# Attention in four query groups of 144 on eight array tiles, with PSUM divided by hand into one region for each stage

## The chip, the cores and the metric

The kernel runs on one core of a Trainium2 chip. The metric is the device time of one execution in microseconds (us). TensorE (PE) multiplies matrices and writes PSUM; VectorE (DVE) and ScalarE (ACT) read PSUM and compute elementwise; GpSimd (POOL) works on SBUF alone; SyncE's queue (SP) starts the DMAs. Each engine works through its own instructions in order and waits at semaphores for the others.

## The reference

Eight batches of eight heads, 576 positions, 64 values a head. Heads 0 to 3 see the 32 positions up to their own, heads 4 to 7 every fourth of the last 128. The attention's output, 4608 rows of 512, goes through a block of two matrix products:

```python
scores = scale * np.matmul(q, k.transpose(0, 1, 3, 2))
scores = np.where(masks[None, :, :, :], scores, -1000000000.0)
attn = softmax(scores)                      # exp, sum, divide
x = (attn @ v).transpose(0, 2, 1, 3).reshape(B * S, H * D)
h = x @ w_in                                # 4608 x 1024
solu = h * softmax(h)
ln = (solu - mean) / sqrt(var + 1e-06) * g_ln
out = ln @ w_out                            # 4608 x 512
```

## The kernel before, in words

**Units and steps.** Attention is cut into 32 units (`n`), two heads of one batch each; units 0 and 1 of a batch have plain heads, units 2 and 3 dilated ones, whose positions the host has regrouped by their remainder modulo 4, so that both kinds need 32 queries against 64 keys at a time. The second block is cut into 36 tiles (`i`) of 128 rows. Units 0 to 3 and the conversion of the weights (float64 bits to two float32r parts, hi and lo) run in a start-up whose order is written out by hand for all engines (`TICKS`). Then come 36 steps, one for each tile. In a step PE computes for tile i `h` (L277, 24 matmuls of 512 columns), for the unit of the step before the product with the values (`attend`, L235), for a new unit the scores (L163), then for tile i-1 the output product `o` (L351, 24 matmuls), and last the eight transposes of tile i (L336). Only PE's order is written by hand in the steps (`LEADS` for the first five, `STEP` for the others); on DVE, ACT and POOL a scheduler places the instructions. A batch is four and a half tiles, so of every nine steps seven have both an `attend` and new scores, one has an `attend` alone and one has scores alone. In steps 2, 5 to 11, 14 to 20 and 23 to 29, 22 in all, the `attend` stands ahead of the scores; steps 31 to 35 have no attention.

**One tile of the second block.** `nmax` (DVE, L288) is the row maximum of `h`, `e` (ACT, L291) the exponential, `t` and `mu` (DVE, L298) their product with `h` and its sum, `t` less its mean follows (L306, L307), and PE transposes it. `th` (ACT, L338) and `tl` (DVE, L339) are the two float32r parts that `o` multiplies. `ob` (ACT, L360) scales the output by `rstd`, which POOL works out in six small instructions (L314 to L321) from two sums.

**One unit of attention.** Queries are stored block-diagonal by head (64 columns for 32 queries of two heads), so one scores matmul has 128 rows, 64 columns of weights and 64 moving columns; 18 of them fill 576 columns in two PSUM tiles (`ps_s0`, `ps_s1`), and two at a time fall on the two halves of the array's columns. DVE adds the mask and takes the maximum (L171, L187), POOL subtracts it (L188), ACT exponentiates (L202), DVE sums, inverts, multiplies (L204 to L214) and transposes blocks of 32 (`pt`, L221). Units 2, 3 and 4 add the mask on PE (L156) and exponentiate straight from PSUM (L197). `attend` has 40 matmuls of 32 rows, 64 columns of weights and up to 64 moving columns, on four tiles of the array, into two PSUM tiles, `ps_x` and `ps_t1`; `ps_t1` is also the tile of the second half of the transposes. `spread` splits each of the two into `x_hi` (ACT, L257) and `x_lo` (DVE, L258), the rows of `h`'s operand.

**PSUM.** Its eight banks hold eight tiles: two for `ps_h`, one each for `ps_o`, `ps_t0`, `ps_t1`, `ps_x`, `ps_s0`, `ps_s1`. A step's waits follow from which instruction reads or writes which of them.

Of the kernel before, what the change touches and what calls it, by code (L numbers as in the profile page):

```python
# [19 lines left out]
NPAIR = H // 2  # L20
# [7 lines left out]
NU = S // WIN // 2  # L28
WQ = 2 * WIN
NV = NU + 1  # L30
KPAD = WIN
RING = 2 * S
HALF = S // 2
# [35 lines left out]
def windowed_attention_then_solu_kernel(  # L69
# [20 lines left out]
    ps_a = ctx.enter_context(tc.tile_pool(name="ps_a", bufs=1, space=PSUM))  # L90
    ps_m = ctx.enter_context(tc.tile_pool(name="ps_m", bufs=1, space=PSUM))
# [9 lines left out]
    mask_sb = const.tile([P, 2, NU, WQ], BF16, name="mask_sb")  # L101
# [8 lines left out]
    x_lo = const.tile([P, KT, RING], F32R, name="x_lo")  # L110
    nc.vector.memset(mhalf, -0.5)
# [28 lines left out]
    def scores(n, part):  # L140

        qt, kt = loaded[n]["q"], loaded[n]["k"]
        dil = int(n % NPAIR >= NPAIR // 2)
        if part == 0:
            st[n] = {"sm": att.tile([P, NU, WQ], F32, name="sm")}
        sm = st[n]["sm"]
        us = range(0, 5) if part == 0 else range(5, NU)
        nu = len(us)
        on_pe = n in PE_MASK
        ps = ps_a.tile([P, 512], F32, name=f"ps_s{part}")  # L150
        ps = ps[:, 0 : 5 * WQ].rearrange("p (u w) -> p u w", w=WQ)
        st[n]["ps", part] = ps
        mk = mask_sb[:, dil, us[0] : us[0] + nu, :]
        if on_pe:
            for c in range(0, P, 64):
                nc.tensor.matmul(  # L156
                    out=ps[c : c + 64, 0:nu, :], lhsT=id_bf[:, c : c + 64], rhs=mk,
                    start=True, stop=False,
                )
        for i, u in enumerate(us):  # L160
            for par in range(2):
                qb = NU * par + u
                nc.tensor.matmul(  # L163
                    out=ps[64 * par : 64 * par + 64, i, :],
                    lhsT=qt[:, qb, :],
                    rhs=kt[:, WIN * qb : WIN * qb + WQ],
                    start=not on_pe,
                    stop=not on_pe or i == nu - 1,
                )
        if not on_pe:  # L170
            nc.vector.tensor_tensor(  # L171
                out=sm[:, us[0] : us[0] + nu, :], in0=ps[:, 0:nu, :], in1=mk, op=ALU.add
            )

    def soft_max(n):
        sm = st[n]["sm"]
        mx = small.tile([P, NU], F32, name="mx")
        if n in PE_MASK:
            st[n]["mx"] = mx
            for part, (u0, u1) in enumerate(((0, 5), (5, 9))):  # L180
                nc.vector.tensor_reduce(
                    out=mx[:, u0:u1], in_=st[n]["ps", part][:, 0 : u1 - u0, :],
                    axis=AX.X, op=ALU.max, negate=True,
                )
# [26 lines left out]
    def soft_norm(n):  # L211
        sm, rs = st[n]["sm"], st[n]["rs"]
        eng = nc.gpsimd if n < NPAIR + POOL_NORM else nc.vector
        eng.tensor_tensor(  # L214
            out=sm, in0=sm, in1=rs.unsqueeze(2).broadcast_to([P, NU, WQ]), op=ALU.mult
        )

    def probs_t(n):

        pt = st[n]["pt"] = att.tile([P, NU * WQ], F32, name="pt")  # L220
        nc.vector.transpose(out=pt, in_=st[n]["sm"].rearrange("p u w -> p (u w)"))  # L221

    def attend(n):

        vt = loaded[n]["v"]
        pt = st[n]["pt"]
        b, pr = divmod(n, NPAIR)
        out = [ps_a.tile([P, 512], F32, name="ps_x"), ps_m.tile([P, 512], F32, name="ps_t1")]
        for i in range(NV):
            u0, u1 = max(i - 1, 0), min(i + 1, NU)  # L230
            k0, k1 = max(WQ * i - WIN, 0), min(WQ * i + WIN, NU * WQ)
            for par in range(2):
                for h in range(2):
                    r = 64 * par + 32 * h
                    nc.tensor.matmul(  # L235
                        out=out[par][64 * h : 64 * h + 64, WIN * u0 : WIN * u1],
                        lhsT=vt[r : r + WIN, i, :],
                        rhs=pt[r : r + WIN, k0:k1],
                        start=i == 0,
                        stop=i == NV - 1,  # L240
                        skip_group_check=True,
                    )
        for half in range(2):
            spread(n, out[half][:, 0:HALF], half)

    def spread(n, ps, half):
        b, pr = divmod(n, NPAIR)
        base = (b % 2) * S

        def view(x):  # L250
            x = x[:, pr, base : base + S]
            if pr < NPAIR // 2:
                return x[:, half * HALF : half * HALF + HALF]
            return x.rearrange("p (i c) -> p c i", c=DIL)[:, 2 * half : 2 * half + 2, :]

        src = ps if pr < NPAIR // 2 else ps.rearrange("p (c i) -> p c i", c=2)
        nc.scalar.copy(out=view(x_hi), in_=src)  # L257
        nc.vector.tensor_tensor(  # L258
            out=view(x_lo), in0=src, in1=view(x_hi).bitcast(F32), op=ALU.subtract
        )  # L260
        if half == 1:
            del st[n], loaded[n]
# [4 lines left out]
    def moe_h(i, half, kts):  # L267
        if half == 0 and kts[0] == 0:
            ms[i] = {"h": ps_m.tile([P, 2, 512], F32, name="ps_h")}
        h = ms[i]["h"]  # L270
# [14 lines left out]
    def moe_act(i):  # L285
        h = ms[i]["h"].rearrange("p a b -> p (a b)")
# [7 lines left out]
    def moe_gate(i):  # L294
        h = ms[i]["h"].rearrange("p a b -> p (a b)")
# [28 lines left out]
    def moe_t():  # L324
# [144 lines left out]
    def front_ops(n):  # L469
        return {  # L470
            "s0": lambda: scores(n, 0),
            "s1": lambda: scores(n, 1),
# [75 lines left out]
def _mask():  # L548
    m = np.full((P, 2, NU, WQ), NEG, np.float32)
    c = np.arange(WQ)  # L550
    for u in range(NU):
        for p in range(P):
            qb = NU * (p // 64) + u
            q = WIN * qb + p % WIN
            k = WIN * (qb - 1) + c
            ok = (k >= 0) & (q - k >= 0) & (q - k < WIN)
            m[p, 0, u, ok] = 0.0
            m[p, 1, u, ok & (k // CLS == q // CLS)] = 0.0
    return m
# [47 lines left out]
```

## Time and profile before

| | |
|---|---|
| median of three runs (lowest to highest) | 576.47 us (576.36 to 577.3) |
| the profiled execution, its span | 577.16 us, 575.1 us |
| mean granted clock of TensorE | 0.967 |
| step with attend and scores, from one nmax to the next | 14.49 or 14.5 us |
| step with attend alone, with scores alone, without attention | 13.29, 13.57, 11.77 us |
| start of the first nmax (end of the start-up) | 61.58 us |

Of the engines' rows: a start, a duration, the engine, the line, the operation, what is written and from what, the shape, and in brackets the idle time ahead of it with what ended it. A matmul's duration includes its way through the array, so matmuls overlap and the distance of their starts tells the rate. The profile merges neighbours ("x36"). A matmul in float32 stands in the trace as two instructions. A table by windows gives for each stretch its length and then, engine by engine, the busy time and the number of instructions, last the granted clock of TensorE, the share of the DMA engines and GB/s.

### The profile page before, as it was taken

How to read it: one execution, taken by the hardware profiler on the slowest of the kernel's cores; microseconds unless marked ns; L12 is line 12 of the kernel's file. 1: busy time of each engine (PE TensorE's matmuls, PEld its weight loads, DVE VectorE, ACT ScalarE, POOL GpSimd, SP SyncE). 2: the span in 40 equal slices, each digit the busy share in tenths (PEclk: the TensorE clock that was granted, in tenths of full speed). 3: DMA queues.
4: the chain of work that ended last, by engine and by line, in shares of the span. 5: the costliest groups of instructions: out<-in, count | busy, mean ns of one | idle time of the engine just before them, and what ended most of it. 6: DMA issues, size and time to landing. Idle time of an engine off the chain costs nothing.

```text
span 575.1 us, 13371 instructions
## 1 busy us (share of the span) xinstructions
PE 531.8 (92%) x5740; PEld 442.2 (77%) x5740; DVE 356.7 (62%) x617; ACT 225.5 (39%) x451; POOL 153.9 (27%) x280
## 2 busy tenths in 40 slices
PE   3464859999999999999999999999999999999996
PEld 2353648888888888888888888888888888888885
DVE  4988995645666666655666666646666666634342
ACT  3467753343333333333333333333333333333232
POOL 2654771212222222211222222211222222211111
PEclk9966779999999999999999999999999999999999
DMA  8786620312333333323232333222333310001000
GB/s 316 233 305 248 200 73 34 106 61 88 103 106 104 105 104 99 103 58 98 96 110 95 106 105 106 98 83 81 114 105 103 96 49 19 19 19 38 18 19 36
DMA packets 22090, 58.40 MB, mean 102 GB/s; under 512 B 2704, under 2 KB 3088, under 8 KB 22032
## 3 DMA queue, kind: packets, MB, share of 16 engines
q1 hardware_dynamic: 22032, 57.55, 30.1%
q8 instruction: 45, 0.74, 0.5%
q14 instruction: 13, 0.11, 0.0%
HBM read 48.11 MB, written 9.44 MB: 100 GB/s over the span
## 4 chain that ended last, share of the span: by engine, by line
PE 83%; DVE 8%; ACT 3%; issue 2%; DMA 2%; POOL 1%; SPq 0%; ACTq 0%; DVEq 0%
PE ps_h L277 34%; PE ps_o L351 32%; PE ps_x L235 5%; PE ps_s L163 5%; PE ps_t L336 5%; DVE mag L399 1%; PE ps_t L235 1%; DVE nmax L288 1%; DVE mag L414 1%; DMA raw<-w_out 1%; DMA mask_sb<-mask 1%; ACT e L291 1%; POOL sm L188 1%; DVE rs L204 1%; DVE mag L407 1%
## 5 line engine op out<-in xcount | busy, mean ns | idle before, releaser
L277 PE MATMUL ps_h<-wi_hi,x_hi 128*128 128x512 f32 x288 | 117.6, 408 | 7.5 <-ACT x_hi L257 5.3
L351 PE MATMUL ps_o<-wo_hi,th 128*128 128x512 f32 x288 | 116.2, 404 | 0.8 <-ACT th L338 0.8
L277 PE MATMUL ps_h<-wi_hi,x_lo 128*128 128x512 f32 x288 | 114.2, 397 | 0.0
L277 PE MATMUL ps_h<-wi_lo,x_hi 128*128 128x512 f32 x288 | 113.7, 395 | 0.0
L351 PE MATMUL ps_o<-wo_hi,tl 128*128 128x512 f32 x288 | 113.1, 393 | 0.0
L351 PE MATMUL ps_o<-wo_lo,th 128*128 128x512 f32 x288 | 113.1, 393 | 0.0
L291 ACT ACTIVATE e<-ps_h,nmax 128x1024 f32<-128x1024 f32 x36 | 40.2, 1116 | 168.2 <-DVE nmax L288 168.2
L288 DVE TENSOR_REDUCE nmax<-ps_h 128x1 f32<-128x1024 f32 x36 | 44.0, 1223 | 81.2 <-PE ps_h L277 81.1
L298 DVE CUSTOM_DVE_ANT_0 t<-ps_h,e 128x1024 f32<-128x1024 f32 x36 | 44.1, 1224 | 41.9 <-ACT e L291 41.9
L277 PEld LDWEIGHTS ps_h<-wi_hi,x_hi 128*128 128x128 f32 x288 | 55.3, 192 | 18.5 <-ACT x_hi L257 6.0
L235 PEld LDWEIGHTS ps_x<-pt,vt 32*64 32x64 f32 x1280 | 44.1, 145 | 31.6 <-issue 19.8
L235 PE MATMUL ps_x<-pt,vt 32*64 32x64 f32 (+1 forms) x1280 | 47.7, 230 | 20.8 <-DVE pt L221 11.4
L314 POOL TENSOR_SCALAR se<-se 128x1 f32<-128x1 f32 x36 | 8.9, 246 | 214.9 <-ACT e L291 214.8
L202 ACT ACTIVATE sm<-sm 128x576 f32<-128x576 f32 x29 | 19.9, 685 | 117.5 <-POOL sm L188 117.5
L351 PEld LDWEIGHTS ps_o<-wo_hi,th 128*128 128x128 f32 x288 | 54.5, 189 | 13.4 <-ACT th L338 1.1
L277 PEld LDWEIGHTS ps_h<-wi_hi,x_lo 128*128 128x128 f32 x288 | 54.9, 190 | 12.7 <-DVE x_lo L258 1.0
L188 POOL TENSOR_TENSOR sm<-sm,mx 128x576 f32<-128x576 f32 x29 | 43.9, 1515 | 75.8 <-DVE mx L187 75.5
L351 PEld LDWEIGHTS ps_o<-wo_hi,tl 128*128 128x128 f32 x288 | 54.5, 189 | 12.0 <-DVE tl L339 0.4
L277 PEld LDWEIGHTS ps_h<-wi_lo,x_hi 128*128 128x128 f32 x288 | 55.3, 192 | 10.2
L351 PEld LDWEIGHTS ps_o<-wo_lo,th 128*128 128x128 f32 x288 | 54.5, 189 | 10.5
L339 DVE TENSOR_TENSOR tl<-ps_t,th 128x512 fp32r<-128x512 f32 x72 | 45.6, 672 | 25.5 <-ACT th L338 25.5
L163 PE MATMUL ps_s<-kt,qt 128*64 128x64 f32 x1152 | 45.9, 239 | 9.8 <-DMA qt<-qT 9.8
(60 smaller groups left out, 756.1 us busy)
## 6 DMA issues: line engine op xcount, KB each, us to landing
qt<-qT SPq DMA_DIRECT2D x32, 576.0 KB, 5.4
vt<-vw SPq DMA_DIRECT2D x32, 320.0 KB, 3.2
kt<-kT SPq DMA_DIRECT2D x32, 304.0 KB, 3.9
out<-ob SPq DMA_DIRECT2D x36, 256.0 KB, 2.0
raw<-w_in SPq DMA_DIRECT2D x8, 512.0 KB, 5.6
raw<-w_out SPq DMA_DIRECT2D x8, 512.0 KB, 4.3
mask_sb<-mask SPq DMA_DIRECT2D x2, 144.0 KB, 5.6
id_sb<-ident SPq DMA_DIRECT2D x1, 64.0 KB, 6.8
```

The source lines that it names most:

```text
L163: nc.tensor.matmul(out=ps[64 * par : 64 * par + 64, i, :], lhsT=qt[:, qb, :], rhs=kt[:, WIN * qb : WIN * qb + WQ], start=not on_pe, stop=n ...
L188: nc.gpsimd.tensor_tensor(out=sm, in0=sm, in1=mx.unsqueeze(2).broadcast_to([P, NU, WQ]), op=ALU.subtract)
L202: nc.scalar.activation(out=sm, in_=sm, func=AF.Exp, scale=0.125)
L235: nc.tensor.matmul(out=out[par][64 * h : 64 * h + 64, WIN * u0 : WIN * u1], lhsT=vt[r : r + WIN, i, :], rhs=pt[r : r + WIN, k0:k1], start= ...
L277: nc.tensor.matmul(out=h[:, half, :], lhsT=a[:, kt, xs], rhs=w[:, kt, ws], start=(kt == 0 and k == 0), stop=(kt == KT - 1 and k == 2),)
L288: nc.vector.tensor_reduce(out=nmax, in_=h, axis=AX.X, op=ALU.max, negate=True)
L291: nc.scalar.activation(out=e, in_=h, func=AF.Exp, bias=nmax, scale=1.0, accum_out=se)
L298: nc.vector.tensor_tensor_reduce(out=t, in0=h, in1=ms[i]["e"], scale=1.0, scalar=0.0, op0=ALU.mult, op1=ALU.add, accum_out=mu,)
L314: nc.gpsimd.tensor_scalar(out=se, in0=se, scalar1=1e-9, scalar2=None, op0=ALU.add)
L336: nc.tensor.transpose(out=ps[:, f, :], in_=t[:, k * P : k * P + P], identity=id_sb)
L339: nc.vector.tensor_tensor(out=tl[:, fs], in0=ps, in1=th[:, fs].bitcast(F32), op=ALU.subtract)
L351: nc.tensor.matmul(out=o, lhsT=a[:, f, :], rhs=w[:, f, :], start=(f == 0 and k == 0), stop=(f == FT - 1 and k == 2),)
```

## The change

**Attention in four groups.** The 576 queries of a head are cut into four groups of 144 (`GQ`), each in five blocks of 32 (`NS`; the last one is half padding), and group c lies on partitions 32c to 32c+31. Queries are stored dense. A scores matmul now has 64 rows (one head), 32 columns of weights and 64 moving columns; there are 40 in a unit, eight at a time on eight tiles of the array (two heads by four groups). `attend` has 48 matmuls of 32 rows in a plain unit and 40 in a dilated one, on eight tiles (four groups by two heads). Arrays of a unit's probabilities grow from 576 to 640 columns. Mask addition, maximum and `spread` become one instruction each where there were two. The loads of a unit are 296 KB of queries (were 576), 312 KB of keys (were 304) and 384 KB of values (were 320).

**PSUM.** One tile of all eight banks is divided by hand. `ps_h` has banks 0 and 1, `ps_o` bank 2, the first half of the transposes bank 3. The second half has columns 0 to 255 of banks 4 and 5, the scores columns 0 to 319 of banks 6 (first head) and 7 (second head), and `ps_x` columns 320 to 463 of banks 4 to 7, one bank for each group. `attend` no longer writes a tile of the transposes.

```diff
-NU = S // WIN // 2
+NG = P // WIN
+GQ = S // NG
+NS = -(-GQ // WIN)
+NV = NS + 1
+SPAN = GQ * (NG - 1) + WIN * NS
...
+    banks = psum.tile([P, 8, 512], F32, name="banks")
+    ps_h = banks[:, 0:2, :]
+    ps_o = banks[:, 2, :]
+    ps_s = banks[:, 6:8, 0 : NS * WQ]
+    ps_x = banks[:, 4:8, NS * WQ : NS * WQ + GQ]
+    ps_t = (
+        banks[:, 3:4, :].rearrange("p b (f q) -> p b f q", q=P),
+        banks[:, 4:6, 0 : 2 * P].rearrange("p b (f q) -> p b f q", q=P),
+    )
...
-        for i, u in enumerate(us):
-            for par in range(2):
-                qb = NU * par + u
-                nc.tensor.matmul(
-                    out=ps[64 * par : 64 * par + 64, i, :],
-                    lhsT=qt[:, qb, :],
-                    rhs=kt[:, WIN * qb : WIN * qb + WQ],
...
+        for i in range(NS):
+            for h in range(2):
+                for c in range(NG):
+                    q0 = GQ * c + WIN * i
+                    nc.tensor.matmul(
+                        out=ps[WIN * c : WIN * c + WIN, h, WQ * i : WQ * i + WQ],
+                        lhsT=qt[D * h : D * h + D, q0 : q0 + WIN],
+                        rhs=kt[D * h : D * h + D, q0 : q0 + WQ],
...
-        out = [ps_a.tile([P, 512], F32, name="ps_x"), ps_m.tile([P, 512], F32, name="ps_t1")]
...
+            for c in range(NG):
                 for h in range(2):
-                    r = 64 * par + 32 * h
                     nc.tensor.matmul(
-                        out=out[par][64 * h : 64 * h + 64, WIN * u0 : WIN * u1],
-                        lhsT=vt[r : r + WIN, i, :],
-                        rhs=pt[r : r + WIN, k0:k1],
+                        out=ps_x[D * h : D * h + D, c, c0 : c0 + k1 - k0],
+                        lhsT=vt[WIN * c : WIN * c + WIN, i, D * h : D * h + D],
+                        rhs=pt[WIN * c : WIN * c + WIN, h, k0:k1],
...
-        for half in range(2):
-            spread(n, out[half][:, 0:HALF], half)
+        spread(n)
...
-        nc.scalar.copy(out=view(x_hi), in_=src)
+        nc.scalar.copy(out=view(x_hi), in_=ps_x)
         nc.vector.tensor_tensor(
-            out=view(x_lo), in0=src, in1=view(x_hi).bitcast(F32), op=ALU.subtract
+            out=view(x_lo), in0=ps_x, in1=view(x_hi).bitcast(F32), op=ALU.subtract
         )
```

**PE in a step.** The rows are the end of an `attend`, the scores and the start of `o` in a step of the middle of the program; in brackets stand the semaphores that an instruction waits for (DMAHW are those of loads). Before:

```order
L235 MATMUL ps_x<-pt,vt 64x32 x2
L235 MATMUL ps_t_3153<-pt,vt 64x32 x2
L163 MATMUL ps_s_3199<-kt,qt 64x64 [waits DMAHW1_49,DMAHW0_49]
L163 MATMUL ps_s_3199<-kt,qt 64x64 x9
L163 MATMUL ps_s_3216<-kt,qt 64x64 x8
L351 MATMUL ps_o<-wo_hi,th 128x512 [waits Activation_49]
L351 MATMUL ps_o<-wo_lo,th 128x512
```

The same place in the changed kernel, where all of PSUM is named `banks` and L239 is `attend`, L167 the scores, L354 `o`:

```order
L239 MATMUL banks<-pt,vt 64x64 [waits DMAHW6_49,DVE_49]
L239 MATMUL banks<-pt,vt 64x64 x23
L239 MATMUL banks<-pt,vt 64x48 x8
L239 MATMUL banks<-pt,vt 64x16 x8
L167 MATMUL banks<-kt,qt 32x64 [waits DMAHW5_49,DMAHW4_49,DVE_49]
L167 MATMUL banks<-kt,qt 32x64 x39
L354 MATMUL banks<-wo_hi,th 128x512 [waits Activation_49]
L354 MATMUL banks<-wo_lo,th 128x512
```

The order on PE is the same; the first matmul of the scores has a wait for DVE that it had not. The count that it waits for is the one that DVE reaches with `x_lo` (L260) of the same step, the instruction that reads what the `attend` just ahead has written.

**DVE and POOL in a step.** DVE before, from the maximum of `h` on:

```order
L288 TENSOR_REDUCE nmax_3736<-ps_h_3650 128x1
L298 ISA t_3759,mu_3760<-ps_h_3650,e_3738 128x1024
L298 ISA mu_3760 128x1
L258 TENSOR_TENSOR x_lo_91<-ps_x_3677,x_hi_90 128x288
L258 TENSOR_TENSOR x_lo_91<-ps_t1_3678,x_hi_90 128x288
L171 TENSOR_TENSOR sm_3723<-ps_s0_3724,mask_sb_82 128x320
L171 TENSOR_TENSOR sm_3723<-ps_s1_3741,mask_sb_82 128x256
L306 TENSOR_SCALAR mu_3760<-mu_3760 128x1
L187 TENSOR_REDUCE mx_3751<-sm_3723 128x9
L307 TENSOR_SCALAR t_3759<-t_3759,mu_3760 128x1024
```

DVE in the changed kernel (L289 is `nmax`, L299 the product with `e`, L260 `x_lo`, L176 the mask addition, L192 the maximum of the scores, L308 the subtraction of the mean):

```order
L289 TENSOR_REDUCE nmax_4091<-banks_89 128x1
L299 ISA t_4104,mu_4105<-banks_89,e_4093 128x1024
L299 ISA mu_4105 128x1
L260 TENSOR_TENSOR x_lo_88<-banks_89,x_hi_87 128x576
L307 TENSOR_SCALAR mu_4105<-mu_4105 128x1
L308 TENSOR_SCALAR t_4104<-t_4104,mu_4105 128x1024
L176 TENSOR_TENSOR sm_4049<-banks_89,mask_sb_79 128x640
L192 TENSOR_REDUCE mx_4096<-sm_4049 128x10
```

POOL in the changed kernel, one step: the three instructions on `se`, then those on `sq` and `rstd`, then the subtraction of the unit's maximum, which stood ahead of `sq` before:

```order
L315 TENSOR_SCALAR se_3900<-se_3900 128x1
L317 TENSOR_TENSOR s2_3918<-se_3900 128x1
L318 TENSOR_SCALAR s2_3918<-s2_3918 128x1
L319 TENSOR_SCALAR sq_3915<-sq_3915 128x1
L320 TENSOR_TENSOR s2_3918<-s2_3918,sq_3915 128x1
L322 TENSOR_TENSOR rstd_3923<-s2_3918,mhalf_82 128x1
L193 TENSOR_TENSOR sm_3855<-sm_3855,mx_3902 128x640
```

On DVE the mask addition and the maximum moved behind the subtraction of the mean; on POOL the subtraction of the maximum moved behind `rstd`; on ACT, in the same steps, the exponential of the scores moved behind the sum of squares.

**PE in the start-up.** The `attend` of unit 1 in the changed kernel, in the order of groups (two matmuls for each group and block):

```order
L239 MATMUL banks<-pt,vt 64x32 [waits DMAHW4_49,DVE_49]
L239 MATMUL banks<-pt,vt 64x32 x3
L239 MATMUL banks<-pt,vt 64x32 [waits Activation_49]
L239 MATMUL banks<-pt,vt 64x32
L239 MATMUL banks<-pt,vt 64x32 [waits Activation_49]
L239 MATMUL banks<-pt,vt 64x32
```

The fifth matmul is the first into bank 6 and the seventh the first into bank 7. Each waits for ACT, for the last exponential of unit 2 that reads columns 0 to 319 of that bank; the `attend` itself writes columns 320 to 463. The four matmuls into banks 4 and 5 have no such wait. In the kernel before, no matmul of an `attend` waits for ACT.

More of the change, by code (lines that the diff above doesn't have):

```diff
@@ L138, in windowed_attention_then_solu_kernel, with scores @@
     st = {}
-    def scores(n, part):
+    def scores(n):
         qt, kt = loaded[n]["q"], loaded[n]["k"]
         dil = int(n % NPAIR >= NPAIR // 2)
[L144 to L148, printed above, removed]
+        ps = ps_s
+        st[n] = {"ps": ps.rearrange("p h (s w) -> p h s w", w=WQ)}
+        sm = st[n]["sm"] = att.tile([P, 2, NS, WQ], F32, name="sm")
@@ new lines, in scores @@
+        for i in range(NS):
+            for h in range(2):
+                for c in range(NG):
[4 more added lines that the diff above has]
+                        rhs=kt[D * h : D * h + D, q0 : q0 + WQ],
+                        start=not on_pe,
+                        stop=True,
+                        skip_group_check=True,
+                    )
@@ L178, in soft_max @@
         if n in PE_MASK:
[L179 to L184, printed above, removed]
+            nc.vector.tensor_reduce(out=mx, in_=st[n]["ps"], axis=AX.X, op=ALU.max, negate=True)
             nc.gpsimd.tensor_scalar(out=mx, in0=mx, scalar1=0.125, scalar2=None, op0=ALU.mult)
@@ L242, in attend, with spread @@
                     )
[L243 to L246 removed]
+        spread(n)
+    def spread(n):
         b, pr = divmod(n, NPAIR)
@@ L268, in moe_h @@
         if half == 0 and kts[0] == 0:
-            ms[i] = {"h": ps_m.tile([P, 2, 512], F32, name="ps_h")}
-        h = ms[i]["h"]
+            ms[i] = {}
+        h = ps_h
         assert reached[-1] >= KT * (half + 1)
@@ L285, in moe_act @@
     def moe_act(i):
-        h = ms[i]["h"].rearrange("p a b -> p (a b)")
+        h = ps_h.rearrange("p a b -> p (a b)")
         nmax = small.tile([P, 1], F32, name="nmax")
@@ L294, in moe_gate @@
     def moe_gate(i):
-        h = ms[i]["h"].rearrange("p a b -> p (a b)")
+        h = ps_h.rearrange("p a b -> p (a b)")
         t = moe.tile([P, DF], F32, name="t", bufs=T_BUFS)
@@ L470, in front_ops @@
         return {
-            "s0": lambda: scores(n, 0),
-            "s1": lambda: scores(n, 1),
+            "s0": lambda: scores(n),
             "max": lambda: soft_max(n),
@@ L548, in _mask @@
 def _mask():
-    m = np.full((P, 2, NU, WQ), NEG, np.float32)
+    m = np.full((P, 2, NS, WQ), NEG, np.float32)
     c = np.arange(WQ)
-    for u in range(NU):
+    for s in range(NS):
         for p in range(P):
[L553 to L559, printed above, removed]
+            q0 = GQ * (p // WIN) + WIN * s
+            q = q0 + p % WIN
+            k = q0 - WIN + c
+            ok = (q >= S) | ((k >= 0) & (q - k >= 0) & (q - k < WIN))
+            m[p, 0, s, ok] = 0.0
+            m[p, 1, s, ok & ((q >= S) | (k // CLS == q // CLS))] = 0.0
+    return m.reshape(P, 2, NS * WQ)
 def _bits(a):
```

125 lines of the change are left out of this document (57 added, 68 removed).

## The prediction

> **What bounds the kernel now.** The page first: PE's share, and the chain that ended last by engine.
>
> ```profile
> span 575.1 us, 13371 instructions
> PE 531.8 (92%) x5740; PEld 442.2 (77%) x5740; DVE 356.7 (62%) x617; ACT 225.5 (39%) x451; POOL 153.9 (27%) x280
> PE 83%; DVE 8%; ACT 3%; issue 2%; DMA 2%; POOL 1%; SPq 0%; ACTq 0%; DVEq 0%
> ```
>
> Then a table by windows for one step in the middle (length, then busy time of PE, PEld, DVE, ACT and POOL, then PE's granted clock):
>
> ```profile
> 303.00:317.50 14.50, 14.50 (x174) 12.15 (x173) 9.66 (x18) 5.56 (x10) 3.68 (x7) 1.00 0.31 108
> ```
>
> PE is never idle in a step, DVE for a third of it. So a step lasts as long as PE's matmuls in it, which the timeline of PE shows:
>
> ```profile
> 311.08 0.39 PE L277 MATMUL ps_h<-wi_hi,x_lo 128*128 128x512 f32 x1
> 311.39 0.24 PE L235 MATMUL ps_x<-pt,vt 32*64 32x32 f32 x2
> ...
> 311.79 0.22 PE L235 MATMUL ps_x<-pt,vt 32*64 32x64 f32 x2
> 311.81 0.22 PE L235 MATMUL ps_t<-pt,vt 32*64 32x64 f32 x2
> 311.85 0.22 PE L235 MATMUL ps_x<-pt,vt 32*64 32x64 f32 x2
> ...
> 312.52 0.23 PE L235 MATMUL ps_x<-pt,vt 32*64 32x32 f32 x2
> ...
> 312.69 1.27 PE L163 MATMUL ps_s<-kt,qt 128*64 128x64 f32 x36
> 313.89 0.50 PE L351 MATMUL ps_o<-wo_hi,th 128*128 128x512 f32 x1
> ...
> 325.57 0.39 PE L277 MATMUL ps_h<-wi_hi,x_lo 128*128 128x512 f32 x1
> ```
>
> The last matmul of h starts at 311.08 (I call it S) and the next step's at 325.57: 14.49 us. In between attend has 311.39 to 312.69 (1.30 us), the scores 312.69 to 313.89 (1.20 us), and o, transposes and h 313.89 to 325.57 (11.68 us). The attention's part is 2.50 us.
>
> **PE's own work.** In attend four matmuls on four array tiles start within 0.02 us (311.79, 311.81) and the next four 0.06 us later (311.85): 80 instructions, 20 rounds. The scores have 36 instructions, two at a time, 18 rounds, also 0.06 us each (1.05 of the 1.20 us, with about 0.15 to change over). After the change a plain attend has 12 rounds of eight and a dilated one 10, the scores 10. If eight tiles run at once as four do, attend saves 8 or 10 rounds (about 0.45 or 0.55 us) and the scores 8 (about 0.45 us, leaving 0.75). That is 0.9 to 1.0 us a step, if PE stays the bound.
>
> Trainium skill, "TensorE: Matmul & The Clock Gate", Part 1, says that matmuls never start closer than about 25 ns, however small; by it the 80 instructions of the new scores would take 2.0 us and speak against the change. The trace disagrees: 80 instructions in 1.13 us (311.39 to 312.52), 14 ns each.
>
> **The wait that the change adds.** The order shows the scores' first matmul waiting for DVE's x_lo of the same step. x_lo reads ps_x in banks 4 to 7, the scores write banks 6 and 7. They share no byte; but in the start-up the waits of attend fall exactly on the matmuls into banks 6 and 7 and not on those into 4 and 5, so the program is guarded bank by bank. PE works in order: behind the waiting matmul stand all scores, then o, the transposes and the next h. Before, x_lo came long after the scores had gone:
>
> ```profile
> 311.50 1.22 DVE L288 TENSOR_REDUCE nmax<-ps_h 128x1 f32<-128x1024 f32 x1 [1.57 <-PE ps_h L277]
> 314.06 1.23 DVE L298 CUSTOM_DVE_ANT_0 t<-ps_h,e 128x1024 f32<-128x1024 f32 x1 [1.33 <-ACT e L291]
> 315.21 0.66 DVE L258 TENSOR_TENSOR x_lo<-ps_x,x_hi 128x288 fp32r<-128x288 f32 x1
> 315.78 0.65 DVE L258 TENSOR_TENSOR x_lo<-ps_t,x_hi 128x288 fp32r<-128x288 f32 x1
> ```
>
> ```profile
> 312.82 1.11 ACT L291 ACTIVATE e<-ps_h,nmax 128x1024 f32<-128x1024 f32 x1 [4.33 <-DVE nmax L288]
> 313.93 0.67 ACT L257 CAST x_hi<-ps_x 128x288 fp32r<-128x288 f32 x1
> 314.38 0.74 ACT L257 CAST x_hi<-ps_t 128x288 fp32r<-128x288 f32 x1
> ```
>
> The chain is h, nmax on DVE, e on ACT, the product t on DVE, and then x_lo (DVE's order after the change still has nmax and t ahead of it, ACT's has e ahead of x_hi). None of that gets shorter: x_lo starts 4.13 us after S (315.21 - 311.08). This unit is dilated and its two x_lo end at 316.43, 1.22 us on. A plain one is quicker:
>
> ```profile
> 329.70 0.45 DVE L258 TENSOR_TENSOR x_lo<-ps_x,x_hi 128x288 fp32r<-128x288 f32 x1
> 330.07 0.45 DVE L258 TENSOR_TENSOR x_lo<-ps_t,x_hi 128x288 fp32r<-128x288 f32 x1
> ```
>
> Here 329.70 is again 4.13 us after its S (325.57), and the end 0.82 us on. One instruction of 576 columns in place of two of 288 saves one start; by the distance of the two starts (0.37 us) against the duration (0.45 us) that is about 0.09 us. So x_lo ends at S + 4.86 (plain) or S + 5.26 (dilated). From DVE's end to PE's start the chain of waits shows 0.04 us:
>
> ```profile
> 81.50 0.70 DVE pt L221
> 82.20 0.04 issue
> 82.24 0.32 PE ps_x L235 x2
> ```
>
> The scores then take 0.78 us and the rest 11.68. Step: 4.86 + 0.04 + 0.78 + 11.68 = 17.36 us plain, 17.76 dilated, against 14.49. Of the 22 steps with attend ahead of the scores 12 have a plain attend and 10 a dilated one: 12 x 2.87 + 10 x 3.27 = **+67 us**. The saved attend vanishes in the wait. The four steps with attend alone (all dilated) and the three with scores alone have no such wait and save 4 x 0.55 + 3 x 0.45, **-3.5 us**.
>
> **The clock.** PE is now idle in each of these steps, from the end of attend at about S + 1.1 to S + 4.9 or 5.3: 3.8 or 4.2 us. What that does to its clock the start-up shows; these stretches are cut where the granted clock changes, in pieces of 3.41 us:
>
> ```profile
> 40.46:43.88 3.42, 3.42 (x85) 3.30 (x75) 2.15 (x5) 2.63 (x14) 1.21 (x1) 0.50 0.77 262
> 43.88:47.29 3.41, 1.37 (x7) 0.48 (x3) 2.08 (x3) 3.25 (x7) 2.57 (x3) 1.00 0.83 288
> 47.29:50.70 3.41, 1.07 (x40) 1.10 (x44) 3.38 (x8) 0.84 (x2) 0.25 (x2) 0.50 0.79 313
> ...
> 54.12:57.53 3.41, 2.60 (x6) 1.74 (x7) 3.38 (x9) 3.41 (x7) 1.16 (x1) 0.50 0.79 261
> 57.53:60.94 3.41, 3.41 (x10) 2.64 (x9) 3.38 (x4) 1.78 (x4) 2.63 (x3) 0.50 0.18 39
> 60.94:64.36 3.42, 3.24 (x119) 2.62 (x117) 3.33 (x5) 2.87 (x5) 3.15 (x3) 1.00 0.79 249
> 64.36:67.77 3.41, 1.35 (x6) 1.05 (x6) 3.41 (x9) 3.40 (x7) 1.22 (x3) 1.00 0.89 311
> 67.77:71.18 3.41, 3.41 (x14) 2.81 (x13) 3.41 (x5) 2.43 (x5) 3.10 (x3) 0.50 0.72 240
> 71.18:74.60 3.42, 3.42 (x16) 2.61 (x14) 3.42 (x6) 2.22 (x5) 3.26 (x5) 1.00 0.01 2
> ```
>
> PE busy for 1.37 or 1.35 of 3.41 us (40%) at full clock is followed by a window at 0.50, and only a fully busy window (3.41, not 2.60) ends that. An idle time of 3.8 us leaves one window with at most 1.5 us of work wherever it falls, so nearly every one of the 22 waits buys a half-speed window. In such a window matmuls of 512 columns are 0.43 us apart, at full clock 0.23 us (the last two rows):
>
> ```profile
> 85.55 0.63 PE L351 MATMUL ps_o<-wo_hi,tl 128*128 128x512 f32 x1
> 85.98 0.63 PE L351 MATMUL ps_o<-wo_hi,th 128*128 128x512 f32 x1
> ...
> 316.06 0.39 PE L351 MATMUL ps_o<-wo_hi,th 128*128 128x512 f32 x1
> 316.29 0.39 PE L351 MATMUL ps_o<-wo_lo,th 128*128 128x512 f32 x1
> ```
>
> So a window full of half-speed work loses 3.41 x (1 - 0.23/0.43) = 1.6 us. Where the wait reaches into the slow window, that window is not full and a second one is slow: about 2.8 us. By the position of the wait in the window, which drifts from step to step, about six in ten lose 1.4 to 1.6 and three to four in ten 2.8, 2.0 on average: 22 x 2.0 = **+44 us** (22 to 60).
>
> **What stays small.** The start-up is set by DVE's conversion of weights; the scores there get the same wait, for x_lo of the unit before, and attend one for the exponentials, while PE's work and the first loads (296 for 576 KB of queries) shrink. No row prices the sum; I take 0, between -6 and +8. On DVE, POOL and ACT 640 for 576 columns adds about 0.07 us to each of some six instructions; they now have three more microseconds a step, so that is hidden.
>
> **Sum.** 577.16 us is the profiled execution (span 575.1), 0.7 above the median of 576.47. 577.2 + 67 - 3.5 + 44 + 0 = 684.7, so 684 for a median.
>
> **Rivals.**
>
> The clock falls only when PE is idle for a whole window. A wait of 3.8 or 4.2 us covers one of 3.41 entirely in one step of nine to one of four, so the loss is 4 x 1.9 = 8 instead of 44 us: 648; with no loss at all 640. Against it: the windows with 40% of work above. The same page of the Trainium skill, Part 1, says that the clock is halved after an idle window and restored after a busy one; by its wording this rival holds, and the 40% rows speak for a threshold above zero. Chance 0.13.
>
> Eight tiles don't run at once, but four. attend's 24 rounds stay hidden in the wait, the scores have 20 rounds, 0.6 us more: 22 x 0.6 = 13, and the seven other steps save nothing: 701. For it: no row has eight tiles or four moving operands on the same rows. Against: starts in a round are 0.02 us apart, far under the 0.06 of a round. Chance 0.12.
>
> The division works as its description reads, stages don't wait for each other, and the step is PE's 14.49 less 0.95: 22 x 0.95 + 3.5 = 24, so 552. DVE would then be near its limit: it idles 1.57 us a step, and loses some of that by the reorder on DVE and POOL (t no longer lies in the wait for POOL, 0.75 us, and the subtraction waits for rstd), which brings it to about 564. It decides if the wait for x_lo falls before S + 1.0; it can't, since x_lo follows nmax, e and t. The Trainium skill's page "PSUM — Partial Sum Buffer", section on bank collisions, demands semaphores by bank and quadrant, not by address; by it a program without this wait would not be sound. Chance 0.04.
>
> **How the numbers follow.** Forecast 684 with 0.71, 648 with 0.13, 701 with 0.12, 564 with 0.04. The forecast's own range, from the clock's 22 to 60 and the start-up, is 660 to 705. The range 641 to 704 takes in the first two rivals. A measurement tells 0.2% (1.2 us): faster 0.04, same 0.01, slower 0.95.
>
> **What would show it.** Right: PE waits on the scores' line for DVE x_lo, 3.8 us in each of 22 steps, about 85 us in all; steps of 18.5 to 20.5 us; windows at clock 0.50 throughout; 13 us steps without the wait. Wrong: no wait there, a mean clock near 0.97 with the wait, or scores that take over 1.1 us at full clock.

## The result, and the profile after

The changed kernel takes 691.64 us (median of 4 runs, 690.43 to 692.74) against 576.41 us before: a ratio of 1.1995, 95% interval 1.1971 to 1.2019. The profiled execution took 692.01 us, its span is 690.2 us. From the page of the changed kernel come the span, the engines' busy shares, PE's granted clock in 40 slices, the chain that ended last by engine, and the group of the scores (after the bar: busy us, mean ns, then PE's idle time ahead of it and what ended most of it):

```profile
span 690.2 us, 16590 instructions
PE 558.7 (81%) x7398; PEld 452.9 (66%) x7398; DVE 369.9 (54%) x553; ACT 230.6 (33%) x425; POOL 138.9 (20%) x280
PEclk9999888998888899999888889999888889999999
PE 71%; DVE 16%; ACT 7%; DMA 2%; issue 1%; POOL 1%; SPq 0%; ACTq 0%
L167 PE MATMUL banks<-kt,qt 64*32 64x64 f32 x2560 | 41.8, 288 | 90.9 <-DVE mu L307 80.6
```

PE's share fell from 92% to 81%, DVE's and ACT's shares of the chain doubled. The waits of PE name the place (total us, times, longest):

```profile
PE banks L167 <- DVE mu L307: 80.6, 22, 4.0
```

22 waits, as many as there are steps with attend ahead of scores. The releaser named is `mu` (L307), the small instruction behind `x_lo`; the count that the scores wait for is that of `x_lo`, and in all 22 steps they start 0.055 to 0.057 us after it has ended. A plain and a dilated step in the timeline, PE and DVE:

```profile
330.06 0.39 PE L278 MATMUL banks<-wi_hi,x_lo 128*128 128x512 f32 x1
330.38 1.20 PE L239 MATMUL banks<-pt,vt 32*64 32x32 f32 x96
...
334.19 0.75 DVE L260 TENSOR_TENSOR x_lo<-banks,x_hi 128x576 fp32r<-128x576 f32 x1
...
335.00 1.40 PE L167 MATMUL banks<-kt,qt 64*32 64x64 f32 x80 [3.43 <-DVE mu L307]
...
349.75 0.39 PE L278 MATMUL banks<-wi_hi,x_lo 128*128 128x512 f32 x1
350.07 1.08 PE L239 MATMUL banks<-pt,vt 32*64 32x64 f32 x80
...
353.88 1.16 DVE L260 TENSOR_TENSOR x_lo<-banks,x_hi 128x576 fp32r<-128x576 f32 x1
...
355.10 1.40 PE L167 MATMUL banks<-kt,qt 64*32 64x64 f32 x80 [3.95 <-DVE mu L307]
```

`x_lo` ends at 334.94 and 355.04, the scores start 0.06 us later. S is 330.06 and 349.75, so the first of these steps takes 19.69 us, where it took 14.49. The chain of waits through the second of them runs through DVE and ACT from 350.18 to 355.11, and PE, done with attend, stands still for 3.95 us of that (start, length, what):

```profile
347.87 2.28 PE banks L278 x10
...
350.18 1.24 DVE nmax L289
...
351.49 1.21 ACT e L292 x2
...
352.73 1.23 DVE t L299
...
353.96 1.08 DVE x_lo L260
...
355.11 1.39 PE banks L167 x76
356.50 7.55 PE banks L354 x24
364.05 0.87 PE banks L337 x8
364.92 5.47 PE banks L278 x24
```

24 matmuls take 7.55 us in `o` and 5.47 us in `h`: the clock. By windows of 3.41 us (busy time of PE, PEld, DVE, ACT and POOL, then PE's granted clock):

```profile
329.79:333.21 3.42, 1.78 (x99) 1.29 (x98) 1.40 (x2) 1.41 (x3) 0.12 (x1) 1.00 0.20 40
333.21:336.62 3.41, 1.62 (x81) 1.45 (x82) 2.73 (x6) 1.06 (x2) 0.52 (x3) 0.50 0.21 80
336.62:340.03 3.41, 3.41 (x9) 2.64 (x9) 1.46 (x2) 0.89 (x3) 2.23 (x4) 0.50 0.59 176
340.03:343.45 3.42, 3.42 (x17) 2.79 (x16) 2.88 (x5) 0.27 (x1) 0.00 (x0) 1.00 0.02 6
```

In the first window the wait begins, the next two are at half clock. Counting those that reach over an edge, the full window at 0.50 holds 9 matmuls of 512 columns, the one behind it 17.

### The profile page after: what moved, and what is told of

It reads as the page before. It is cut to its first block, busy times and chain, and to the rows that moved or that the text cites. A ratio compares the mean times of both kernels' runs of the same rounds, so it can differ in the third digit from the quotient of the medians.

```text
span 690.2 us, 16590 instructions
## 1 busy us (share of the span) xinstructions
PE 558.7 (81%) x7398; PEld 452.9 (66%) x7398; DVE 369.9 (54%) x553; ACT 230.6 (33%) x425; POOL 138.9 (20%) x280
## 4 chain that ended last, share of the span: by engine, by line
PE 71%; DVE 16%; ACT 7%; DMA 2%; issue 1%; POOL 1%; SPq 0%; ACTq 0%
PE banks L354 34%; PE banks L278 27%; PE banks L167 5%; DVE nmax L289 4%; PE banks L337 4%; ACT e L292 4%; DVE t L299 4%; DVE x_lo L260 3%; ACT sm L201 1%; PE banks L239 1%; DVE mag L402 1%; DMA raw<-w_in 1%; DMA raw<-w_out 1%; DVE mag L417 1%; DMA g_sb<-g_ln 1%
## 5 line engine op out<-in xcount | busy, mean ns | idle before, releaser
L354 PE MATMUL banks<-wo_hi,th 128*128 128x512 f32 x288 | 132.9, 461 | 0.8 <-ACT th L345 0.8
L354 PE MATMUL banks<-wo_lo,th 128*128 128x512 f32 x288 | 126.4, 439 | 0.0
L354 PE MATMUL banks<-wo_hi,tl 128*128 128x512 f32 x288 | 124.6, 433 | 0.0
L278 PE MATMUL banks<-wi_hi,x_hi 128*128 128x512 f32 x288 | 117.4, 408 | 5.8 <-ACT x_hi L259 5.8
L167 PE MATMUL banks<-kt,qt 64*32 64x64 f32 x2560 | 41.8, 288 | 90.9 <-DVE mu L307 80.6
L278 PE MATMUL banks<-wi_hi,x_lo 128*128 128x512 f32 x288 | 114.3, 397 | 0.3 <-DVE x_lo L260 0.3
L278 PE MATMUL banks<-wi_lo,x_hi 128*128 128x512 f32 x288 | 113.7, 395 | 0.0
L289 DVE TENSOR_REDUCE nmax<-banks 128x1 f32<-128x1024 f32 x36 | 44.0, 1223 | 123.2 <-PE banks L278 123.2
L167 PEld LDWEIGHTS banks<-kt,qt 64*32 64x32 f32 x2560 | 34.8, 135 | 96.5 <-DVE mu L307 82.7
L354 PEld LDWEIGHTS banks<-wo_hi,th 128*128 128x128 f32 x288 | 63.7, 221 | 18.7 <-issue 3.2
L354 PEld LDWEIGHTS banks<-wo_hi,tl 128*128 128x128 f32 x288 | 62.7, 218 | 15.7 <-DVE tl L346 0.4
L354 PEld LDWEIGHTS banks<-wo_lo,th 128*128 128x128 f32 x288 | 63.9, 222 | 13.1
L299 DVE CUSTOM_DVE_ANT_0 t<-banks,e 128x1024 f32<-128x1024 f32 x36 | 44.1, 1224 | 43.1 <-ACT e L292 43.1
L239 PE MATMUL banks<-pt,vt 32*64 32x64 f32 (+3 forms) x2816 | 41.7, 239 | 26.7 <-DVE pt L223 17.3
L239 PEld LDWEIGHTS banks<-pt,vt 32*64 32x64 f32 x2816 | 37.2, 142 | 39.2 <-DVE pt L223 18.9
L278 PEld LDWEIGHTS banks<-wi_lo,x_hi 128*128 128x128 f32 x288 | 55.1, 191 | 10.1
```

Source lines behind the costliest of these rows:

```text
L167: nc.tensor.matmul(out=ps[WIN * c : WIN * c + WIN, h, WQ * i : WQ * i + WQ], lhsT=qt[D * h : D * h + D, q0 : q0 + WIN], rhs=kt[D * h : D * ...
L239: nc.tensor.matmul(out=ps_x[D * h : D * h + D, c, c0 : c0 + k1 - k0], lhsT=vt[WIN * c : WIN * c + WIN, i, D * h : D * h + D], rhs=pt[WIN * ...
L278: nc.tensor.matmul(out=h[:, half, :], lhsT=a[:, kt, xs], rhs=w[:, kt, ws], start=(kt == 0 and k == 0), stop=(kt == KT - 1 and k == 2),)
L289: nc.vector.tensor_reduce(out=nmax, in_=h, axis=AX.X, op=ALU.max, negate=True)
L299: nc.vector.tensor_tensor_reduce(out=t, in0=h, in1=ms[i]["e"], scale=1.0, scalar=0.0, op0=ALU.mult, op1=ALU.add, accum_out=mu,)
L354: nc.tensor.matmul(out=o, lhsT=a[:, f, :], rhs=w[:, f, :], start=(f == 0 and k == 0), stop=(f == FT - 1 and k == 2),)
```

## The experiments

Each kernel is compared with the kernel before on the same chip. Theory A is the prediction's: the scores wait for `x_lo` because both use banks 6 and 7, and the idle time brings half-clock windows. Rival B: the new attention itself is slower. Rival C: the wait costs, the clock does not follow it.

**The wait alone, in the kernel before** (`wait_alone`):

```diff
-        ps = ps_a.tile([P, 512], F32, name=f"ps_s{part}")
+        late = part == 0 and n > NPAIR
+        ps = ps_a.tile([P, 512], F32, name="ps_x" if late else f"ps_s{part}")
```

> The kernel before with one change: from unit 5 on the first part of the scores is written into the PSUM tile of attend (ps_x), so that the scores wait for x_lo of the same step; shapes, array tiles, queries and loads stay. Theory A (the scores' wait for x_lo costs the time, and the half-clock windows that the idle time brings double it): the first x_lo ends 4.58 us (plain) or 4.79 us (dilated) after S, plus 0.04, plus scores 1.20, plus 11.68 = 17.50 or 17.71 us a step, 12 x 3.01 + 10 x 3.22 = 68 us for the waits, and 2.0 to 2.4 us of clock in each of 22 steps, 44 to 53: 577 + 68 + 48 = 693 us, between 688 and 700, mean clock about 0.91. Rival B (the new attention itself, with eight tiles, more and smaller matmuls and arrays of 640 columns, is the slower one): 577 us. Rival C (the wait costs, the clock does not follow it): 645 us, mean clock 0.96.

Measured 694.87 us, ratio 1.2058 (1.2002 to 1.2114), clock 0.899. In its waits, and in a plain step, the releaser is `x_lo` itself:

```profile
PE ps_x L164 <- DVE x_lo L259: 67.0, 22, 3.2
```

```profile
305.06 0.39 PE L278 MATMUL ps_h<-wi_hi,x_lo 128*128 128x512 f32 x1
...
309.19 0.45 DVE L259 TENSOR_TENSOR x_lo<-ps_x,x_hi 128x288 fp32r<-128x288 f32 x1
...
309.69 1.34 PE L164 MATMUL ps_x<-kt,qt 128*64 128x64 f32 x20 [2.95 <-DVE x_lo L259]
```

`x_lo` ends 4.58 us after S, as expected to the hundredth, and the scores start 0.05 us later. This kernel has none of the new attention, and is as slow as the changed one. Rival B falls as the cause of the loss, and C misses by 50 us.

**The wait filled with work** (`filled_wait`): `fill(14)` stands between attend and scores in the 21 steps that the common order makes; step 2 has an order of its own and is left as it is.

```diff
+    def fill(k):
+        for _ in range(k):
+            nc.tensor.matmul(
+                out=ps_o, lhsT=wo_hi[:, 0, 0:P], rhs=wo_hi[:, 0, :], start=True, stop=True
+            )
```

> The changed kernel with 14 extra matmuls of 512 columns into ps_o between attend and scores in each of the 22 steps with both; nobody reads their result, the first matmul of o overwrites it. They take 14 x 0.23 = 3.2 us, less than the wait of 3.8 to 4.2 us, so the scores start when they did. Theory A: the wait for x_lo stays, but no window is nearly idle, the half-clock windows of these steps go: 692 - 22 x 2.35 = 640 us, between 632 and 650, mean clock 0.96 or more; step 17.4 or 17.8 us. Rival C (the clock has nothing to do with it, the steps are long for another reason) and rival B: 692 us, or more by what the extra work costs.

Measured 652.08 us, ratio 1.1306 (1.1286 to 1.1327), clock 0.987, a little above the expected 632 to 650. More work for PE, 39.6 us less time. A dilated step, PE's rows with DVE's `x_lo`, L491 being the filling:

```profile
332.29 0.39 PE L278 MATMUL banks<-wi_hi,x_lo 128*128 128x512 f32 x1
332.61 1.08 PE L239 MATMUL banks<-pt,vt 32*64 32x64 f32 x80
333.62 3.47 PE L491 MATMUL banks<-wo_hi 128*128 128x512 f32 x14
...
336.42 1.16 DVE L260 TENSOR_TENSOR x_lo<-banks,x_hi 128x576 fp32r<-128x576 f32 x1
...
337.64 1.04 PE L167 MATMUL banks<-kt,qt 64*32 64x64 f32 x80 [0.55 <-DVE mu L307]
338.61 0.50 PE L354 MATMUL banks<-wo_hi,th 128*128 128x512 f32 x1
...
350.29 0.39 PE L278 MATMUL banks<-wi_hi,x_lo 128*128 128x512 f32 x1
```

The scores still start when `x_lo` has ended, 5.35 us after S (337.64 - 332.29), and `o` to `h` again takes 11.68 us (350.29 - 338.61). Rival C falls: what went is the clock's part alone. The 12 us over the expected 640 are the clock's share too: it was put at 2.35 us in 22 steps and is 1.92 us in 21. The steps are 17.6 and 18.0 us long, 0.2 more than expected: the scores take 0.97 us (338.61 - 337.64), not 0.78.

**Half of the filling** (`half_filled`), `fill(7)` in place of `fill(14)`:

> The changed kernel with 7 extra matmuls in each wait in place of 14: PE is idle for about 2.3 (plain) or 2.7 us (dilated) of each such step in place of 0.6 and 4. If the clock falls only after a window that is wholly idle, none falls: 652 us as with 14. If it falls after any window that is less than half busy (the rows of the start-up with 40%, those of the changed kernel with 45%), the idle time makes such a window when at least 1.7 us of it lie in one window of 3.41 us: about 8 in 10 steps, 22 x 0.8 x 1.9 = 33 us: 685 us. If the share that decides lies lower, between: 660 to 675 us.

Measured 662.81 us (one run), clock 0.954: between the two ends. Two pairs of windows of this kernel (columns as above):

```profile
303.86:307.27 3.41, 1.80 (x45) 1.19 (x45) 2.31 (x5) 1.56 (x3) 0.64 (x3) 1.00 0.36 115
307.27:310.68 3.41, 3.41 (x71) 2.85 (x59) 2.05 (x3) 1.15 (x2) 1.52 (x4) 1.00 0.43 109
...
358.47:361.88 3.41, 1.30 (x81) 1.17 (x82) 3.09 (x6) 1.21 (x2) 0.45 (x3) 1.00 0.18 69
361.88:365.30 3.42, 3.42 (x10) 2.63 (x9) 1.42 (x2) 0.95 (x3) 2.20 (x4) 0.50 0.61 182
```

A window with 1.80 us of work keeps the clock, one with 1.30 loses it. Over the kernels the two overlap: in the changed kernel windows with 1.78 and 1.87 us (from 493.63) lost it, in `wait_alone` one with 1.75 us (from 145.32) kept it. What decides lies at about half a window of work. (The ends of matmuls are modelled, so it can't be read closer.) The expectation had this share right but the idle time wrong: PE waits 1.60 us in a plain step and 2.14 in a dilated one, not 2.3 and 2.7. A wait of 1.60 us leaves at least 1.81 us of a window for work, and all 12 plain steps keep the clock (17.6 us); of the nine dilated ones six lose it (19.6 us) and three keep it (18.0), where eight steps in ten were expected to lose. So 662.81 lies in the range that was meant for a lower share, without the share being lower.

**The wait hidden by another order on PE** (`o_ahead`, changed kernel) and its control (`before_o_ahead`, kernel before): six of the eight slices of `o` go between attend and scores (`oa`), and the later `o` does the two that are left.

```diff
+OA = 6
...
+            moe_o(done[0], range(part[0], upto))
+            part[0] = upto % FT
+            done[0] += upto == FT
...
+        ops["oa"] = lambda: finish(OA)
...
-    "h0 t0 h1 t1 h2 t2 h3 x0 x1 s0 act s1 max exp inv gate var lv lq norm o t"
+    "h0 t0 h1 t1 h2 t2 h3 x0 x1 oa s0 act s1 max exp inv gate var lv lq norm o t"
```

> The changed kernel with another order on PE: of the eight slices of o of the tile before, six (18 matmuls, 4.1 us) stand between attend and scores, two behind the scores. Nothing else is changed. The x_lo that the scores wait for ends 4.9 or 5.3 us after S, the six slices end 5.2 us after S. Theory A: the wait is gone, PE is busy throughout, full clock: 555 us if PE bounds (13.55 us a step), up to 573 us if DVE's chain bounds the step at 14.1 to 14.4 us. Rival B: the new attention is as slow as it was, 650 us or more. Rival C gives the same as A here.

> Control: the kernel before with the same order on PE (six of eight slices of o between attend and scores, two behind). There the scores wait for nobody, so theory A and C expect no change: 577 us, between 574 and 580, steps of 14.5 us. If the order by itself brings something (or costs something, because the scores come 4 us later and the chain to pt gets shorter of time), the time moves by the same amount as in the changed kernel, and that amount has to be taken off there.

Measured 578.78 us, ratio 1.0038 (1.0023 to 1.0052); control 580.99 us, 1.0076 (1.0052 to 1.01). So 113 us of the 115 go with an order that takes nothing out. But the gain that was left is small, and both runs lie above what was expected (555 to 573, 574 to 580): step 2 kept its wait here (20.15 us), and the steps are longer than 13.55 us. A dilated step of `o_ahead`:

```profile
301.59 0.39 PE L279 MATMUL banks<-wi_hi,x_lo 128*128 128x512 f32 x1
301.91 1.08 PE L240 MATMUL banks<-pt,vt 32*64 32x64 f32 x80
302.92 0.50 PE L355 MATMUL banks<-wo_hi,th 128*128 128x512 f32 x1
...
307.22 1.04 PE L168 MATMUL banks<-kt,qt 64*32 64x64 f32 x80
308.19 0.50 PE L355 MATMUL banks<-wo_hi,th 128*128 128x512 f32 x1
```

attend takes 1.01 us (302.92 - 301.91) where it took 1.30, the scores 0.97 where they took 1.20: 0.52 us saved, not 0.95. The split of `o` costs 0.22 of that (the control's steps are 14.71 us, not 14.49). The step is 14.2 us dilated and 14.35 plain, where attend takes 1.13 us.

**The same order in step 2 too** (`o_ahead_all`); in `o_ahead` step 2 had kept the wait:

```diff
-    "p t h0 h1 t0 h2 t1 h3 t2 x0 s0 act s1 x1 max p exp inv lv norm gate lq t var",
+    "p t h0 h1 t0 h2 t1 h3 t2 x0 x1 oa s0 act s1 max p exp inv lv norm gate lq t var",
```

> Six of eight slices of o between attend and scores in all 22 steps with both: step 2, whose order is written out separately and which kept the wait in the first such run (20.16 us there against 14.49 in the kernel before), now too. Theory A: step 2 falls to 14.3 or 14.5 us, the rest stays: 578.8 - 5.7 = 573 us, between 571 and 575, 0.6% faster than before. If step 2 was long for a reason of the start-up: 578.8 us.

Measured 572.5 us, ratio 0.9923 (0.9904 to 0.9943): faster than both kernels, by 0.8% against the kernel before. Step 2 takes 14.22 us. The wait is gone from PE's waits; on the scores' line there is only that for the first loads:

```profile
PE banks L168 <- DMA qt<-qT: 9.5, 2, 5.0
```

**Scores behind the whole of `o`** (`scores_behind_o`, and `before_scores_behind_o` as control), to save the split:

```diff
-    "h0 t0 h1 t1 h2 t2 h3 x0 x1 s0 act s1 max exp inv gate var lv lq norm o t"
+    "h0 t0 h1 t1 h2 t2 h3 x0 x1 o s0 act s1 max exp inv gate var lv lq norm t"
```

> The changed kernel with the scores behind the whole of o, just ahead of the transposes, in every step with both and in step 2 too (where the run with six slices of o ahead still had the wait). Without a wait and without an extra change between o and scores the step is PE's work: from the run with six slices, 14.20 (dilated) and 14.35 us (plain) less the 0.22 us that the split of o cost the kernel before, so 13.98 and 14.13. Theory A: 22 steps save 12 x 0.36 + 10 x 0.51 = 9.4 us, the seven other steps 2.7, the start-up loses 3: 577 - 9 = 568 us, between 565 and 573. Rival: the scores come so late (7 us after S) that the chain of mask, maximum, exponential, sum, product and transposition ends after the next attend should start, by up to 1 us: 14.5 to 15 us a step, 577 to 590 us.

> Control: the kernel before with the same order on PE, scores behind the whole of o. There is no wait to remove and PE's work is the same: 577 us, between 575 and 580, if the chain to pt is in time; more if it is not, which then counts for the changed kernel too.

Measured 584.88 us, ratio 1.0136 (1.0112 to 1.0159); control 579.02 us, 1.0041 (1.0025 to 1.0056). The rival came true. `pt` ends after PE has reached the next attend, which waits for it in each of these steps:

```profile
316.49 0.85 DVE L223 STREAM_TRANSPOSE pt<-sm 128x640 f32<-128x640 f32 x1
...
317.39 0.82 PE L239 MATMUL banks<-pt,vt 32*64 32x64 f32 x58 [0.50 <-DVE pt L223]
```

Steps are 14.72 and 14.85 us; 0.5 us of that is the wait for `pt`. The control's steps are 14.65 us, 0.16 more than before, so this place isn't free either.

**Scores ahead of attend** (`scores_ahead`), with one slice of `o` between:

```diff
-    "h0 t0 h1 t1 h2 t2 h3 x0 x1 s0 act s1 max exp inv gate var lv lq norm o t"
+    "h0 t0 h1 t1 h2 t2 h3 s0 oa x0 act max exp inv gate var lv lq norm o t"
```

> The changed kernel with the other order of the two users of banks 6 and 7: the scores directly behind h, then one slice of o (3 matmuls), then attend, then the rest of o; in step 2 too. Now attend waits for the mask addition of the same step (the reader of the scores), which follows nmax: S + 1.35 + 0.82 = S + 2.2, while PE reaches attend at S + 0.32 + 0.97 + 0.8 = S + 2.1. Theory A (a short wait costs its length and no clock): 14.3 and 14.45 us a step, 573 us, between 569 and 579, clock full in these steps. If any wait at all on the shared banks brings half-clock windows, 590 us or more.

Measured 581.0 us, ratio 1.008 (1.0055 to 1.0105), above what was expected. Most steps are 14.42 or 14.52 us and the clock stays at 1.00. The mask addition ends 0.21 us after attend has started, and attend takes 0.2 us longer (1.20 us dilated, 1.01 in `o_ahead`): here a short wait costs its length. But five of 22 steps took 15.05 to 15.55 us; in the one below attend is broken by an idle time that nothing in the profile releases:

```profile
302.15 1.09 PE L240 MATMUL banks<-pt,vt 32*64 32x64 f32 x67
303.91 0.32 PE L240 MATMUL banks<-pt,vt 32*64 32x16 f32 x13 [0.66 <-issue]
```

What these gaps are, stays open; they are worth about 4 us.

**Twice the scores' instructions** (`scores_twice`):

```diff
-        for i in range(NS):
+        for i in [*range(NS)] * (1 + (n > NPAIR)):
```

> What 80 more of the scores' instructions cost: the kernel with six slices of o ahead of the scores, and from unit 5 on the 40 matmuls of the scores are issued twice over, the second time into the same places (the values stay). If eight tiles work at the rate that the first 32 starts of a group show (eight in 0.058 us), a step with scores grows by 10 x 0.058 = 0.58 us. If the rate of the later starts holds (about 12 ns for each instruction, however many tiles), it grows by 80 x 0.012 = 0.96 us or a little more. Four tiles at once would give 20 x 0.058 = 1.16 us.

```profile
307.70 1.79 PE L168 MATMUL banks<-kt,qt 64*32 64x64 f32 x160
309.42 0.50 PE L355 MATMUL banks<-wo_hi,th 128*128 128x512 f32 x1
```

606.57 us (one run). The scores take 1.72 us (309.42 - 307.70) for 160 instructions, 0.75 more than for 80: 9.4 ns each, between the two rates that were put up. So eight tiles are faster than four (14 ns each for attend in the kernel before), but not twice as fast. (Three of the 22 steps are 1.7 to 1.9 us longer than the others of this run; PE waits there on the scores' line for nothing that the profile shows.)

**Attend first in the start-up** (`startup_attend_first`, on top of `o_ahead_all`; three orders of the start-up changed like this one):

```diff
-    "A F G B C lv s0 s1 B max D G E C t0 t1 t2 D lq exp inv x0 norm x1 A E",
+    "A F G B C lv s0 s1 B max D G E C t0 t1 t2 x0 D lq exp inv norm x1 A E",
```

> The run with o ahead in all 22 steps, and in the start-up the attend of units 1, 2 and 3 stands ahead of the exponentials of the next unit, so that its matmuls into banks 6 and 7 no longer wait for exponentials that read other columns of those banks. Theory A (the start-up loses its 3 us to this wait): the third nmax starts at about 98 in place of 101 us, 569 to 570 us in all. Rival (the start-up's DVE chain loses them elsewhere, or the exponentials now wait and cost the same): 572.5 us or more.

Measured 582.83 us, ratio 1.0102 (1.0085 to 1.0119), 10 us more than `o_ahead_all`; the third nmax starts at 112.07 us, not at 98. The 6.4 us that attend waited for exponentials are gone, but DVE now waits 5.2 us for exponentials and 6.3 for `x_hi` (2.1 and 3.6 in `o_ahead_all`). The order is worse for another reason than the one that it was to test, so what the start-up loses in the changed kernel is not settled by it.

## Why the prediction was right, point by point

684 was forecast, in a range of 641 to 704; 691.64 came. The direction, the place and the totals of both large terms held; each term was off by 1 to 5 us. Against the span before, 115.1 us more:

| term | forecast | measured | from |
|---|---|---|---|
| waits of 22 steps | +67 | about +72 | 21 steps: 17.6 or 18.0 us in `filled_wait` against 14.49, 68.9; step 2 adds 3 to 3.5, estimated as the others |
| clock in these steps | +44 | about +43 | steps of the changed kernel less those of `filled_wait`, 1.92 each over the 21, so 40.3; the rest of step 2's +5.7 |
| seven lighter steps | -3.5 | -2.7 | 13.0 for 13.29, 13.06 for 13.56 |
| start-up | 0 (-6 to +8) | +3.0 | third nmax at 101.32, not 98.36 |

**The wait.** `x_lo` ends at S + 4.88 (plain, 334.94 - 330.06) and S + 5.29 (dilated, 355.04 - 349.75), forecast 4.86 and 5.26: a chain whose parts keep their durations can be added up from the trace of before. PE stands still for 3.4 and 3.95 us, 80.6 us in all, not for 3.8 and 4.2 (about 85), because attend ends later than was thought; this costs nothing, since the scores start with the end of `x_lo`. That the guard goes by banks, read from which matmuls had waits in the start-up, holds: the changed kernel's scores, which share no byte with `ps_x`, wait 22 times for the count of `x_lo`. (`wait_alone` shows the price of that wait, not the guard: there the two share their bytes.) The Trainium skill's page "PSUM — Partial Sum Buffer", section on bank collisions, asks for a guard by bank and quadrant of partitions, not by address. The trace agrees with the part on banks, in that the program's waits fall so; what the chip does without them, no run here shows. Quadrants could not have helped, since `x_lo` reads all 128 partitions of both banks.

**The clock.** 2.0 us a step were forecast, 1.92 measured, and that they lie so near is partly luck. Six steps in ten were to lose 1.4 to 1.6 us, the others 2.8. Of the 21 steps, nine have one window at 0.50 and lose 1.1 to 1.6 us, and twelve have two and lose 2.0 to 2.7: more steps with two slow windows, each loss smaller. The prediction's rule that only a fully busy window ends the slow state is also too strict; windows with 2.92 to 2.99 us of work ended it in the changed kernel (from 251.29 and 578.97). The rival in which only a wholly idle window counts (648) is out: the windows with 1.78 and 1.30 us of work lost the clock. That is also where the Trainium skill, "TensorE: Matmul & The Clock Gate", Part 1, is too narrow for this trace: it lets the clock fall after an idle window.

**Eight tiles.** This is the step that failed: "If eight tiles run at once as four do". In the sum the scores had 0.78 us (the working above it gives 0.75) and take 0.97 at full clock, which makes 0.19 of each long step, 4 us of the 7.6 that were missing. Neither the forecast nor its rival (four tiles at once) is true. The recorded starts of the scores' matmuls in `o_ahead` show both rates, in us, eight in a line; of the ten lines the first five and the seventh are shown:

```
307.223 .230 .236 .243 .250 .256 .263 .270
307.303 .310 .316 .323 .330 .336 .343 .350
307.359 .366 .372 .379 .386 .392 .399 .406
307.415 .421 .428 .435 .441 .448 .455 .461
307.491 .546 .555 .571 .588 .605 .621 .632
...
307.706 .716 .722 .732 .739 .750 .755 .766
```

The first starts of the third and fourth line are 0.056 us apart: eight at once, 7 ns a start. Behind the 33rd the distances are 2 to 18 ns, after a first one of 55 ns, and the 48 starts from 307.491 to 308.046 are 12 ns apart on average. Why the rate falls there, no run shows; `scores_twice` shows only that 80 more cost 9.4 ns each. So the gain of the change, without its wait, is 0.52 us a step (0.3 to 0.4 plain), not 0.95.

**The fourth rival** (564, no wait) gave the right idea of what was left, but not the size: with the wait hidden 572.5 was reached. What it lacked is the rate of the tiles, the 0.22 us a step for splitting `o`, and the start-up, whose third nmax is 2.6 us late there (100.94 against 98.36). Its sentence that DVE idles 1.57 us a step counts only the wait ahead of `nmax`: the prediction's own window has DVE busy for 9.66 of 14.50 us.

**What stays open.** The start-up's 3 us; the gaps in `scores_ahead` and `scores_twice`; why the rate falls behind the 32nd start.

## What to carry to other kernels

PSUM that is divided without a shared byte is still shared where two stages use one bank: before such a division is chosen, write down for each bank who reads it last and which engine's next instruction writes it, and add up the chain between them. In these kernels a wait on PE costs more than its length if it leaves less than about half of a 3.41 us window of work; move independent work into the wait (here part of the tile's output product, 113 us), and run the same order on the kernel before, so that the order's own price (here 0.22 us a step) isn't booked on the change. Where small matmuls on many tiles are to save time, price them by the rate of a long run of them, not by that of the first 32.

## What the runs showed of the hardware that was not expected

The clock fell behind windows of 3.41 us that were far from idle: it was lost with up to 1.98 us of PE work (`half_filled`, from 64.92) and kept with as little as 1.75 (`wait_alone`, from 145.32), so the two overlap at a little over half. At half clock much more than half is needed to end it: in `wait_alone` one with 2.88 us of work at 0.50 was followed by another at 0.50, and the full one behind that by 1.00 (in the changed kernel 2.92 us sufficed):

```profile
309.16:312.57 3.41, 2.88 (x38) 2.66 (x39) 2.68 (x9) 1.15 (x2) 0.31 (x2) 0.50 0.01 5
312.57:315.98 3.41, 3.41 (x10) 2.64 (x9) 1.40 (x2) 0.68 (x1) 1.80 (x3) 0.50 0.78 264
315.98:319.40 3.42, 3.42 (x17) 2.74 (x16) 1.93 (x4) 0.00 (x0) 0.00 (x0) 1.00 0.00 0
```

The other is the rate above: 32 instructions start about 7 ns apart on eight tiles, those behind them 12 on average. The Trainium skill, "TensorE: Matmul & The Clock Gate", Part 1, has about 25 ns as the least distance of two starts, by which 80 would take 2.0 us; the trace has 0.97.
